# An FFT convolution kernel whose head computes the filter before it transforms the first pixels

## The chip, the core and the metric

The kernel runs on one core of a Trainium2 chip. The core has five engines that run their own instruction streams and meet through semaphores: TensorE (PE in the profile, with its weight loads shown apart as PEld), VectorE (DVE), ScalarE (ACT), GpSimd (POOL) and SyncE (SP), which here issues the DMAs. TensorE writes only into PSUM, eight banks of 512 fp32 columns on each partition; VectorE or ScalarE has to copy every result out ("evict" it) before a bank can be used again. The metric is the device time of one execution in microseconds (us).

## What is computed

The reference is a circular 7 by 7 convolution of a 224 by 224 image with 96 input and 96 output channels, written with two-dimensional FFTs:

```python
# x: (1, 224, 224, 96) bf16, w: (7, 7, 96, 96) bf16
wp = jnp.pad(w, ((0, H - K), (0, W - K), (0, 0), (0, 0)))
Xf = rfft2(x.astype(float32), axes=(1, 2))
Wf = rfft2(wp.astype(float32), axes=(0, 1))
Yf = jnp.einsum('bhwi,hwio->bhwo', Xf, Wf)
y = irfft2(Yf, s=(H, W), axes=(1, 2)).astype(bfloat16)
```

## The kernel before

The kernel does not take a full FFT. It cuts the image rows into 8 blocks of 28 (`NJ`, `B`), takes a short real transform along the rows in each block (34 input rows with overlap, 17 frequencies `s`, a real and an imaginary plane each), convolves along the columns directly in that domain, and transforms back. The columns go in 7 tiles `t` of 32.

Four kinds of work pass through TensorE.

- *The pixel transform.* `f_jobs` and `a_bank` multiply pixels (stationary, `x0_bufs` for tile 0, `xn_bufs` later) by the transform matrix `Fm` (moving) into `xf`. For tiles 0 to 2 the work is split by frequency in three parts, `SH2 = (0, 8, 13, 17)`: 8, 5 and 4 frequencies, 32 matmuls for each part and each half `jg` of the image rows, of 64, 40 and 32 columns. `xh` is the strip of six columns left of tile 0.
- *The filter transform.* `w` lies in `wq` (`wqx`) with its 49 taps on partitions, in two copies: rows 30 to 78 (first copy, all output channels) and rows 79 to 127 (second copy, shifted by 48 output channels, with the other half of the output channels in it). A matmul with `wq` as stationary operand, read with a stride of 96 elements, and a small matrix `Em` as the moving one gives the filter at some frequencies for one output channel. The first group of frequencies uses the first copy alone (`wide_jobs`, line 396: rows 0 to 78, one output channel per matmul); the others use both copies (`prep_jobs`, line 414: one matmul gives two output channels). `PGRP` lists the groups. Results go to `WF`. Of a frequency's three filter planes two are computed and the third is their difference, a VectorE instruction (`diff`, line 389).
- *The convolution.* `b_round` (line 555) handles one frequency of one tile: 33 matmuls of 96 columns (22 at the two real frequencies), with planes of `xf` and of `J` (sums and differences of `xf`, made on VectorE by `jit`, line 525) as stationary and `WF` as moving operands. Its results pass ScalarE (`tt_`), VectorE (`u`, `v`) and GpSimd (`yf`) and go to DRAM.
- *The inverse transform* (`c_jobs`), which starts much later.

The order of every engine's instructions is the order in which the Python emits them (`_Ordered`, line 91). The program has a head (lines 202 to 384 and 758 to 778) and then rounds `r`. In round `r`, tile 0 handles frequency `r` and, from round 4 on, tile 1 frequency `r - 4`. Each `b_round` has two places where other work is slipped in (`mid` and `end`), and the slots are numbered `k`: tile 0 alone has slots `2r` and `2r + 1`. `add(a, b, jobs)` spreads a list of jobs evenly over the slots from `a` to `b` (`pace`, line 785). `evac` (line 132) gives each eviction to VectorE or ScalarE by adding up estimated costs.

The head before, in order. SP issues (lines 202 to 211): tile 0's first pixel half, the first filter copy (row 49 apart, in `load_last`, the other 48 rows in one DMA), the two strips, tile 0's second half, tile 1's pixels, and last the second filter copy in four DMAs of 49 rows each. A DMA waits until the eighth before it has landed. TensorE runs 14 matmuls on zeros, transforms tile 0's first half for all 17 frequencies (96 matmuls), then runs 24 blocks of the wide filter work, each of four matmuls into one bank, 128 columns per matmul of which 110 are used (`NB0 = 4`, `NW0 = 11`), with one matmul on zeros after every fourth block (`FEV`); after block 14 (`WMID`) it puts the strips and the first part of the second half in between. Part two and three of the second half go into slots 1 to 6. VectorE and GpSimd meanwhile build `Fm`, `Em` and, on GpSimd alone, the inverse matrix `G` (`build_g`, line 339), which ScalarE and GpSimd finish at the end of the head (`g_fin`, line 777).

Of the kernel before, what the change touches and what calls it, by code (L numbers as in the profile page):

```python
# [9 lines left out]
F32 = mybir.dt.float32  # L10
# [3 lines left out]
KT = 7  # L14
# [14 lines left out]
NB0 = 4  # L29
# [4 lines left out]
PGRP = ((0, 5), (5, 8), (8, 11), (11, 14), (14, 17))  # L34
# [8 lines left out]
CQ = {2: (11, 0), 3: (11, 3), 4: (8, 7), 5: (4, 11), 6: (0, 11)}  # L43
SH2 = (0, 8, 13, 17)
# [3 lines left out]
FILL = 3  # L48
FEV = 4
WMID = 14  # L50
JIT0 = 20
W1 = 30
ZA = 1000
ZB = 3600
# [3 lines left out]
S5 = ((0, 1), (2, 3, 4), (5, 6, 11), (7, 8, 12), (9, 10, 13))  # L58
NW0 = 11


def slot(s, part):
    return S5[s][part] if s < len(S5) else 2 + 3 * (s - 1) + part


@with_exitstack
def kernel(
# [17 lines left out]
    assert K1 + PW == EP and len(S5) == PGRP[0][1]  # L85
# [26 lines left out]
    ps0_cm = tc.tile_pool(name="ps0", bufs=8, space=bass.MemoryType.PSUM)  # L112
    pools = {"psb": ps0_cm.__enter__()}
# [55 lines left out]
    Em = wqx[0:EP, WE:WE + 2 * NSLOT * NTAP].rearrange("p (h a t) -> p h a t", h=2, a=NSLOT)  # L169
# [31 lines left out]

    load_x(0, 0)
    load_last(K1 - 1, 0)
    load_w(W1, 0, PW - 1, 0)
    for jg in range(2):
        load_rows(xh_bufs[jg], jg, W - PAD, PAD)
    load_x(0, 1)
    for jg in range(2):
        load_x(1, jg)
    for i in range(4):  # L210
        load_w(K1, 0, PW, 1, i * WC // 4, (i + 1) * WC // 4)
# [5 lines left out]
    def warm(n):  # L217
        pwu = bank()
        for _ in range(n):
            TE.matmul(pwu[:].rearrange("p (a b) -> p a b", a=4), lhsT=wu[:, 0:128], rhs=wur, start=True, stop=True)  # L220
    warm(7)
    warm(7)

# [14 lines left out]
    pi_t = ftile([128, 1])  # L238
    VE.memset(pi_t[:], math.pi)
    dmy = ftile([128, 1])  # L240
    SE.activation(out=dmy[:], in_=pi_t[:], func=ACTF.Sin, bias=0.0, scale=0.0)
# [5 lines left out]
    zero_a(EP, WE // 2 + NSLOT * NTAP, 64 * C)  # L247
    zero_a(W1, 0, ZA)

# [17 lines left out]
    VE.scalar_tensor_tensor(out=tap[:], in0=ha[:], scalar=-float(PW), in1=pw_i[:], op0=ALU.mult, op1=ALU.add)  # L267
    floor_div(VE, thp[:], tap[:], KT)
# [9 lines left out]
    SE.activation(out=qq[:], in_=qq[:], func=ACTF.Sin, bias=pi_t[:], scale=-2.0 * math.pi / Q)  # L278
    zero_a(W1, ZA, ZB)

    GE.memset(mf[:], 1.0)
    GE.affine_select(out=mf[:], in_=mf[:], pattern=[[-B, JG], [0, NS * 2]], compare_op=ALU.is_ge, fill=0.0, base=-1, channel_multiplier=1)
    GE.affine_select(out=mf[:], in_=mf[:], pattern=[[B, JG], [0, NS * 2]], compare_op=ALU.is_ge, fill=0.0, base=LC, channel_multiplier=-1)
    GE.memset(mf[:, :, 2 * NS - 2:], 0.0)
# [7 lines left out]
    iota(twc[:], [[1, KT]])  # L292
    twp = ftile([EP, 1]); mk = ftile([EP, NTAP]); mk2 = ftile([EP, 2, NTAP])
    th7 = ftile([EP, 1])
    GE.tensor_single_scalar(out=th7[:], in_=thp[:], scalar=-float(KT), op=ALU.mult)
    GE.tensor_tensor(out=twp[:], in0=th7[:], in1=tap[:], op=ALU.add)
    GE.tensor_scalar(out=mk[:, 0:KT], in0=twc[:], scalar1=twp[:, 0:1], scalar2=None, op0=ALU.is_equal)
    GE.tensor_tensor(out=mk[:, KT:NTAP], in0=mk[:, 0:6:2], in1=mk[:, 1:6:2], op=ALU.add)
    VE.scalar_tensor_tensor(out=hm[:, 0:1], in0=hb[:], scalar=-2.0, in1=ha[:], op0=ALU.mult, op1=ALU.add)
    VE.scalar_tensor_tensor(out=hm[:, 1:2], in0=pw_i[:], scalar=float(PW), in1=hm[:, 0:1], op0=ALU.is_ge, op1=ALU.subtract)  # L300
    for h in range(2):
        GE.tensor_scalar(out=mk2[:, h], in0=mk[:], scalar1=hm[:, h:h + 1], scalar2=None, op0=ALU.mult)
# [4 lines left out]

# [9 lines left out]
    for r, k in ((0, KT - 1), (1, 0)):  # L317
        VE.tensor_single_scalar(out=pv[:, NS - 2, r:r + 1], in_=thp[:], scalar=float(k), op=ALU.is_equal)
# [441 lines left out]
    for p in range(3):  # L760
        for f in fj[p][0]:
            f()
# [211 lines left out]
```

## Time and profile before

| what | value |
|---|---|
| median of 3 runs (lowest, highest) | 267.96 us (267.83, 268.06) |
| the profiled execution's own time | 267.92 us |
| its span, first to last instruction | 266.1 us |
| PE busy | 254.9 us (96%), 5128 matmuls |
| DVE busy | 216.2 us (81%) |
| ACT busy | 197.3 us (74%) |
| POOL busy | 98.3 us (37%) |
| DMA | 46.78 MB, mean 176 GB/s |

Times in the views are us from the start of the span, and durations of single instructions are given in ns. A row such as `pb<-WF,J 96*128 96x96` is a matmul that writes the PSUM tile `pb` from the moving operand `WF` (96 partitions by 96 columns) and the stationary operand `J` (96 by 128). `x14` is a number of instructions, and a bracket at the end of a row says how long the engine sat idle before it and what released it. The views name all lines L101, since one helper records every instruction, so rows are told apart by their tiles.

### The profile page before, as it was taken

How to read it: one execution, taken by the hardware profiler on the slowest of the kernel's cores; microseconds unless marked ns; L12 is line 12 of the kernel's file. 1: busy time of each engine (PE TensorE's matmuls, PEld its weight loads, DVE VectorE, ACT ScalarE, POOL GpSimd, SP SyncE). 2: the span in 40 equal slices, each digit the busy share in tenths (PEclk: the TensorE clock that was granted, in tenths of full speed). 3: DMA queues.
4: the chain of work that ended last, by engine and by line, in shares of the span. 5: the costliest groups of instructions: out<-in, count | busy, mean ns of one | idle time of the engine just before them, and what ended most of it. 6: DMA issues, size and time to landing. Idle time of an engine off the chain costs nothing. (4 is left out here: it accounts for less than half of the span.)

```text
span 266.1 us, 12141 instructions
## 1 busy us (share of the span) xinstructions
PE 254.9 (96%) x5128; PEld 235.7 (89%) x5128; DVE 216.2 (81%) x465; ACT 197.3 (74%) x485; POOL 98.3 (37%) x152
## 2 busy tenths in 40 slices
PE   8997999999999999999999999999999999999992
PEld 3887999999998999999999998989999889879871
DVE  7997799889899688778887888777889889878623
ACT  8797977597964577988988789886987854178123
POOL 7781333455557344322223322233123332422100
PEclk9999999999999999999999999999999999999999
DMA  8973103711111697898876587979678533887855
GB/s 200 244 203 110 48 2 93 221 47 47 47 51 47 198 261 159 248 275 231 273 199 192 142 247 218 234 219 345 214 147 235 184 118 136 200 239 185 260 126 188
DMA packets 46786, 46.78 MB, mean 176 GB/s; under 512 B 35272, under 2 KB 38004, under 8 KB 46684
## 3 DMA queue, kind: packets, MB, share of 16 engines
q1 hardware_dynamic: 44444, 43.95, 58.8%
q10 hardware_dynamic: 2288, 2.06, 2.4%
q8 instruction: 40, 0.66, 1.1%
q14 instruction: 14, 0.11, 0.1%
HBM read 24.66 MB, written 21.33 MB: 173 GB/s over the span
## 5 line engine op out<-in xcount | busy, mean ns | idle before, releaser
L101 PE MATMUL pb<-WF,J 96*128 96x96 bf16 x2821 | 162.9, 206 | 1.7 <-DVE J L101 1.3
L101 PEld LDWEIGHTS <-J 96*128 96x128 bf16 x2821 | 138.0, 98 | 12.3 <-issue 3.5
L101 POOL TENSOR_TENSOR yf<-v,u 128x384 bf16<-128x384 f32 x79 | 81.4, 1040 | 145.3 <-issue 84.5
L101 ACT CAST xf<-pb 96x408 bf16<-96x408 f32 (+3 forms) x145 | 67.3, 487 | 6.1 <-PE pb L101 2.3
L101 PE MATMUL pb<-WF,xf 96*128 96x96 bf16 x952 | 60.0, 206 | 0.9 <-ACT WF L101 0.9
L101 DVE TENSOR_TENSOR J<-xf 96x1824 bf16<-96x1824 bf16 (+1 forms) x84 | 56.9, 716 | 0.0
L101 PEld LDWEIGHTS <-xf 96*128 96x128 bf16 x952 | 47.2, 98 | 1.4 <-issue 1.2
L101 PE MATMUL pb<-Fm,xn 118*128 118x136 bf16 (+3 forms) x640 | 45.5, 199 | 0.2 <-DVE u L101 0.2
L101 PE MATMUL pb<-tt,Gm 102*84 102x384 bf16 (+1 forms) x132 | 32.9, 326 | 0.6 <-ACT J L101 0.3
L101 ACT CAST WF<-pb 96x480 bf16<-96x480 f32 (+1 forms) x58 | 28.6, 560 | 3.1 <-PE pb L101 3.1
L101 PEld LDWEIGHTS <-xn 118*128 118x128 bf16 x640 | 30.3, 97 | 0.3 <-issue 0.3
L101 ACT CAST J<-pb 84x384 bf16<-84x384 f32 (+1 forms) x65 | 28.1, 492 | 2.6 <-PE pb L101 2.6
L101 ACT CAST yo<-pb 84x384 bf16<-84x384 f32 (+1 forms) x63 | 27.1, 488 | 2.3 <-POOL yf L101 1.3
L101 DVE TENSOR_TENSOR J<-J 96x912 bf16<-96x912 bf16 (+2 forms) x42 | 24.2, 576 | 0.0
L101 PE MATMUL pb<-wq 128*128 128x120 bf16 (+1 forms) x288 | 21.8, 226 | 1.6 <-DMA wq<-in_w_dram 1.6
L101 PEld LDWEIGHTS <-wq 128*128 128x128 bf16 (+1 forms) x288 | 19.9, 148 | 2.5 <-issue 1.2
L101 DVE TENSOR_TENSOR yf<-v,u 128x384 bf16<-128x384 f32 x26 | 15.1, 581 | 0.9
L101 PE MATMUL pb<-wu 128*112 128x384 bf16 (+1 forms) x59 | 14.7, 396 | 1.1 <-DVE ct L101 1.1
L101 PEld LDWEIGHTS <-wu 128*112 128x112 bf16 (+1 forms) x59 | 7.4, 128 | 5.8 <-issue 3.5
L101 PEld LDWEIGHTS <-Gm 102*84 102x84 bf16 (+1 forms) x132 | 11.1, 117 | 1.0 <-issue 0.4
L101 ACT COPY xf<-xf 96x816 bf16<-96x816 bf16 (+3 forms) x20 | 11.1, 616 | 0.0
L101 ACT CAST tt<-pb 112x384 bf16<-112x384 f32 x8 | 3.6, 479 | 8.7 <-PE pb L101 8.6
(387 smaller groups left out, 239.9 us busy)
## 6 DMA issues: line engine op xcount, KB each, us to landing
scr<-yf SPq DMA_DIRECT2D x30, 288.0 KB
xn<-in_x_dram SPq DMA_DIRECT2D x12, 672.0 KB
tt<-scr SPq DMA_DIRECT2D x24, 336.0 KB
out_dram<-yo SPq DMA_DIRECT2D x12, 252.0 KB
out_dram<-J SPq DMA_DIRECT2D x12, 252.0 KB
tt<-scr SPq DMA_DIRECT2D x6, 288.0 KB
WF<-in_x_dram SPq DMA_DIRECT2D x2, 672.0 KB
out_dram<-tt SPq DMA_DIRECT2D x8, 168.0 KB
```

The source lines that it names most:

```text
L101: r = fn(*a, **k)
```

## The change

The head is put in another order, and with it go other sizes.

- SP issues the first filter copy first, in three DMAs of a third of the columns each with row 49's two small DMAs between them (`load_copy`), then tile 0's first half, the strips, tile 0's second half, then the second filter copy in the same five pieces, and tile 1's pixels last.
- The wide filter group has four frequencies (`NW0 = 8` planes, 80 columns) in place of five. It is made in 8 blocks of 12 matmuls, each into a PSUM tile of two banks that one instruction evicts. The other groups are 4 to 6, 7 to 9, 10 to 12 and 13 to 16; the last has four frequencies, 160 columns per matmul and 16 blocks of three matmuls.
- `HEAD` gives the order: four wide blocks, the first pixel half, a block, a strip, a block, a strip, two blocks, the second pixel half. Only six frequencies of both halves are transformed there (`SH0`; 64 matmuls of 48 columns), evicted from two-bank tiles; the seven and the four others go to slots 0 to 3 and 8 to 11 for both halves. The head has 16 matmuls on zeros at its start and one before each block but the first.
- `Em` becomes `Em0` and `Em2`, both inside the tail of `wq`. `Em0`, `Em2` and then `Fm` are made in that order, GpSimd makes the tap masks `mk2` earlier, and the zeros of rows 0 to 29 of `wq` are written by ScalarE in halves of the output channels.
- The scratch of `build_g` lies in `J_bufs[2]`, and `g_fin` moves to round 3.
- The first `J` subtraction is cut in two (`cuts`), the `diff` of frequency 1 is an instruction in place of columns of the wide matmuls, and the slots of tile 1's first transform and of the filter groups move.

```diff
-NB0 = 4
+NB0 = 12
...
-PGRP = ((0, 5), (5, 8), (8, 11), (11, 14), (14, 17))
+PGRP = ((0, 4), (4, 7), (7, 10), (10, 13), (13, 17))
...
+SH0 = (0, 6, 13, 17)
 SH2 = (0, 8, 13, 17)
...
-FILL = 3
-FEV = 4
-WMID = 14
-JIT0 = 20
+HEAD = ("w", "w", "w", "w", "x0", "w", "h0", "w", "h1", "w", "w", "x1")
 W1 = 30
-ZA = 1000
-ZB = 3600
+ZC = 48
...
-S5 = ((0, 1), (2, 3, 4), (5, 6, 11), (7, 8, 12), (9, 10, 13))
-NW0 = 11
+S4 = ((0, 1), (2, 3, 8), (4, 5, 9), (6, 7, 10))
+NW0 = 8
...
+    psh_cm = tc.tile_pool(name="psh", bufs=4, space=bass.MemoryType.PSUM)
+    pools = {"ps": psh_cm.__enter__()}
...
 
+    def load_copy(p, h):
+        n = (C * C, WC)[h]
+        for i in range(3):
+            load_w(p, 0, PW - 1, h, i * n // 3, (i + 1) * n // 3)
+            if i == 1:
+                load_last(p + PW - 1, h)
+
+    load_copy(W1, 0)
     load_x(0, 0)
-    load_last(K1 - 1, 0)
-    load_w(W1, 0, PW - 1, 0)
     for jg in range(2):
         load_rows(xh_bufs[jg], jg, W - PAD, PAD)
     load_x(0, 1)
+    load_copy(K1, 1)
     for jg in range(2):
         load_x(1, jg)
-    for i in range(4):
-        load_w(K1, 0, PW, 1, i * WC // 4, (i + 1) * WC // 4)
...
         for _ in range(n):
-            TE.matmul(pwu[:].rearrange("p (a b) -> p a b", a=4), lhsT=wu[:, 0:128], rhs=wur, start=True, stop=True)
-    warm(7)
-    warm(7)
+            TE.matmul(pw[:, 0].rearrange("p (a b) -> p a b", a=4), lhsT=wu[:, 0:128], rhs=wur, start=True, stop=True)
+    warm(8)
+    warm(8)
...
+
+    def zero_h(h, c0, c1):
+        zv = wz[0:W1, 0:WE // 2].rearrange("p (i o) -> p i o", o=C2)[:, c0:c1, h * C2 // 2:(h + 1) * C2 // 2]
+        return SE.copy(out=zv, in_=zf[0:W1, 0:1].unsqueeze(2).to_broadcast([W1, c1 - c0, C2 // 2]))
+    zero_a(EP, WE // 2, 64 * C)
+    zero_h(0, 0, ZC)
...
-
+    SE.activation(out=qq[:], in_=qq[:], func=ACTF.Sin, bias=pi_t, scale=-2.0 * math.pi / Q)
+    zero_h(0, ZC, C)
+    late_zero = zero_h(1, 0, C)
...
+    iota(twc[:], [[1, KT]])
     GE.memset(mf[:], 1.0)
     GE.affine_select(out=mf[:], in_=mf[:], pattern=[[-B, JG], [0, NS * 2]], compare_op=ALU.is_ge, fill=0.0, base=-1, channel_multiplier=1)
     GE.affine_select(out=mf[:], in_=mf[:], pattern=[[B, JG], [0, NS * 2]], compare_op=ALU.is_ge, fill=0.0, base=LC, channel_multiplier=-1)
+    twp = ftile([EP, 1]); mk = ftile([EP, NTAP]); mk2 = ftile([EP, 2, NTAP])
+    th7 = ftile([EP, 1])
+    GE.tensor_single_scalar(out=th7[:], in_=thp[:], scalar=-float(KT), op=ALU.mult)
+    GE.tensor_tensor(out=twp[:], in0=th7[:], in1=tap[:], op=ALU.add)
+    GE.tensor_scalar(out=mk[:, 0:KT], in0=twc[:], scalar1=twp[:, 0:1], scalar2=None, op0=ALU.is_equal)
+    GE.tensor_tensor(out=mk[:, KT:NTAP], in0=mk[:, 0:6:2], in1=mk[:, 1:6:2], op=ALU.add)
+    for h in range(2):
+        GE.tensor_scalar(out=mk2[:, h], in0=mk[:], scalar1=hm[:, h:h + 1], scalar2=None, op0=ALU.mult)
...
+        VE.tensor_single_scalar(out=pv[:, NS - 2, r:r + 1], in_=thp[:], scalar=float(k), op=ALU.is_equal)
+    late = [late_zero]
+    for h in range(2):
+        late.append(VE.tensor_tensor(out=Em2[:, h].rearrange("p s (r t) -> p s r t", t=NTAP),
+                                     in0=pw3[:, N4:, 0:2].unsqueeze(3).to_broadcast([EP, NS - N4, 2, NTAP]),
+                                     in1=mk2[:, h].unsqueeze(1).unsqueeze(1).to_broadcast([EP, NS - N4, 2, NTAP]), op=ALU.mult))
     VE.tensor_tensor(out=Fm.rearrange("p r s j -> p j s r"), in0=qq[0:R, 0:JG],
                      in1=mf.rearrange("p j (s r) -> p j s r", r=2), op=ALU.mult)
...
+        at = [8]
+
+        def gtile(shape):
+            n = math.prod(shape[1:])
+            v = J2f[0:shape[0], at[0]:at[0] + n]
+            at[0] += n
+            assert at[0] <= JN // 2
+            return v.rearrange("p (j m) -> p j m", j=nj) if len(shape) > 2 else v
...
     def wide_jobs():
         ncol = NW0 * NTAP
-        wcol = 512 // NB0
-        assert ncol <= wcol and C % NB0 == 0
...
             def f():
-                pw = bank()
-                pv_ = pw[:].rearrange("p (k q) -> p k q", q=wcol)
-                ev = Em[0:K1, 0].rearrange("p a t -> p (a t)")[:, 0:wcol]
-                o0 = ob * NB0
+                pw = psum_tile()
+                ev = Em0[0:K1]
+                if ob:
+                    warm(1, pw)
                 for k in range(NB0):
-                    TE.matmul(pv_[:, k], lhsT=wqx[0:K1, o0 + k:o0 + k + 127 * C + 1:C], rhs=ev, start=True, stop=True)
-                wv = WF[0:C, 0:NW0].rearrange("i a t o -> i (a t) o")
-                apart(("W", 0), ob, evac(wv[..., o0:o0 + NB0], pv_[0:C, :, 0:ncol].rearrange("i k q -> i q k"), NB0 * ncol))
+                    o = ob * NB0 + k
+                    m = TE.matmul(pw[:, k // nk, k % nk * ncol:(k % nk + 1) * ncol], lhsT=wqx[0:K1, o:o + 127 * C + 1:C],
+                                  rhs=ev, start=True, stop=True)
+                    if (ob + 1) * NB0 <= C2:
+                        for z in late:
+                            tc.declare_no_dep(m.ins, z.ins, reason="other output channels")
+                wv = WF[0:C, 0:NW0].rearrange("i a t o -> i (a t) o")[..., ob * NB0:(ob + 1) * NB0]
+                apart(("W", 0), ob, evac(wv.rearrange("i q (b k) -> i q b k", b=2),
+                      pw[0:C, :, 0:nk * ncol].rearrange("i b (k q) -> i q b k", q=ncol), NB0 * ncol))
             return f
         return [mk_(ob) for ob in range(C // NB0)]
...
+    def head_x(jg):
+        s1 = SH0[1]
+        fv = Fm[:, :, 0:s1].rearrange("p r s j -> p r (s j)")
+        n = 2 * s1 * JG
+        for ph in range(2):
+            pa = psum_tile()
+            for k in range(TW):
+                i = 2 * k + ph
+                TE.matmul(pa[:, k // 8, k % 8 * 64:k % 8 * 64 + n], lhsT=xbuf(0, jg)[:, i * C:i * C + 128], rhs=fv, start=True, stop=True)
+            xo = xf0[0:C, ph, :, 0:s1, HALO:HALO + TW, jg * JG:(jg + 1) * JG]
+            pi = pa[0:C].rearrange("c b (w q) -> c (b w) q", q=64)[:, :, 0:n].rearrange("c w (r s j) -> c r s w j", r=2, s=s1)
+            apart(("A", 0), (0, jg, ph, 0), evac(xo, pi, TW * n))
+
+    def head_h(jg):
+        pa = psum_tile()
+        for ph in range(2):
+            a_mm(pa[:, ph], xh_bufs[jg], ph, HALO)
+        a_put(0, xf0, pa, slice(0, 2), HALO, jg, 0)
...
-        assert NB * ncol <= 512 and C2 % hb == 0
+        nb = C // (NB if 2 * ncol * (NB // 2) <= 512 else 6)
+        hb = C2 // nb
...
-        return [mk_(ob) for ob in range(nb)] + [diff(s) for s in range(s0, s1) if s not in REAL]
+        return [mk_(ob) for ob in range(nb)] + [diff(s) for s in range(s0, s1) if s not in REAL and gi > 1]
...
     def f_jobs(t, part):
-        s0, s1 = SH2[part], SH2[part + 1]
+        s0, s1 = (SH2 if t else SH0)[part:part + 2]
...
+        cuts = ((0, 1), (1, n)) if t == g == 0 else ((0, n),)
         return [
-            sub(Jb[:, 0:4, 0:n].rearrange("c (k r) s q -> c k r s q", r=2), dpl,
-                x0.unsqueeze(1).to_broadcast([C, 2, 2, n, PP]), ALU.subtract, 4 * PP * n),
+            sub(Jb[:, 0:4, a:b].rearrange("c (k r) s q -> c k r s q", r=2), dpl[:, :, :, a:b],
+                x0[:, :, a:b].unsqueeze(1).to_broadcast([C, 2, 2, b - a, PP]), ALU.subtract, 4 * PP * (b - a)) for a, b in cuts] + [
...
     xf0 = new_xf(0)
-    fj = [f_jobs(0, p) for p in range(3)]
-    for p in range(3):
-        for f in fj[p][0]:
-            f()
-    warm(FILL)
-    for i, f in enumerate(wide_jobs()):
-        if i == WMID:
-            for jg in range(2):
-                for g in a_bank(0, xf0, xh_bufs[jg], 0, 3, jg, 0):
-                    g()
-            for g in fj[0][1]:
-                g()
-        f()
-        if i == JIT0:
-            for g in jit(0, 0):
-                g()
-        if i % FEV == FEV - 1:
-            warm(1)
-    g_fin()
+    fj = [None] + [f_jobs(0, p) for p in (1, 2)]
+    load["a"] += 300
+    wj = wide_jobs()
+    for h in HEAD:
+        if h == "w":
+            wj.pop(0)()
+        else:
+            (head_x if h[0] == "x" else head_h)(int(h[1]))
+    assert not wj
+    for g in jit(0, 0):
+        g()
+    psh_cm.__exit__(None, None, None)
+    ps0_cm = tc.tile_pool(name="ps0", bufs=8, space=bass.MemoryType.PSUM)
+    pools["psb"] = ps0_cm.__enter__()
...
     for gi in range(1, len(PGRP)):
-        add(4 if gi == 1 else 2 * PGRP[gi - 1][0], 2 * PGRP[gi - 1][1] - 1, prep_jobs(gi))
+        add(3 if gi == 1 else 2 * PGRP[gi - 1][0], 2 * PGRP[gi - 1][1] - 1, prep_jobs(gi))
...
         if r == 0:
-            for i in range(2, PGRP[0][1]):
-                add(2 * i - 4, 2 * i - 3, [diff(i)])
-            add(1, 4, fj[1][1])
-            add(3, 7, fj[2][1])
+            for i in range(1, PGRP[0][1]):
+                add(max(2 * i - 3, 0), 2 * i - 1, [diff(i)])
+            for i in range(*PGRP[1]):
+                add(2 * i - 2, 2 * i, [diff(i)])
+            add(0, 4, fj[1][0] + fj[1][1])
+            add(8, 12, fj[2][0] + fj[2][1])
+        if r == 2:
+            new_xf(1, SH2[0], SH2[1])
         for p in range(3):
-            if r == (1, 3, 5)[p]:
-                new_xf(1, SH2[p], SH2[p + 1])
+            if r == (1, 3, 6)[p]:
+                if p:
+                    new_xf(1, SH2[p], SH2[p + 1])
+                else:
+                    xf_tiles[1] = xf_bufs[1]
                 fj = f_jobs(1, p)
                 if p == 2:
                     for jg in range(2):
                         fj[jg][-1] = then_load(fj[jg][-1], 2, jg)
-                add(2 * r + 1, 2 * r + (5, 5, 4)[p], fj[0] + fj[1])
+                add((4, 7, 12)[p], (7, 11, 15)[p], fj[0] + fj[1])
...
+        if r == 3:
+            g_fin()
```

## The prediction

> **What bounds the kernel now.** I read first the page's busy shares in 40 slices, which say where an engine is full; one slice is 6.65 us.
>
> ```profile
> PE   8997999999999999999999999999999999999992
> DVE  7997799889899688778887888777889889878623
> ACT  8797977597964577988988789886987854178123
> PEclk9999999999999999999999999999999999999999
> ```
>
> TensorE is full at full granted clock everywhere but at the end and in the first 30 us. Time can be won only where PE waits or does work nobody needs; work moved from the head into the rounds is paid for in full. Next, TensorE's instructions in order of time, from the head:
>
> ```profile
> 1.05 5.58 PE L101 MATMUL pb<-wu 128*128 128x512 bf16 x14 [1.05 <-DVE ct L101]
> 6.47 2.69 PE L101 MATMUL pb<-Fm,WF 118*128 118x64 bf16 x96
> 9.01 0.81 PE L101 MATMUL pb<-wu 128*128 128x512 bf16 x3
> 10.28 1.18 PE L101 MATMUL pb<-wq 79*128 79x128 bf16 x16 [0.47 <-DMA wq<-in_w_dram]
> ...
> 18.98 0.38 PE L101 MATMUL pb<-wu 128*128 128x512 bf16 x1
> 20.26 0.50 PE L101 MATMUL pb<-WF,xf 96*128 96x96 bf16 x8 [0.90 <-ACT WF L101]
> ...
> 26.35 0.92 PE L101 MATMUL pb<-wq 128*128 128x120 bf16 x12 [1.11 <-DMA wq<-in_w_dram]
> 27.10 0.63 PE L101 MATMUL pb<-Fm,xn 118*128 118x64 bf16 x16
> ```
>
> The first convolution starts at 20.26, after waiting 0.90 us for the last eviction of wide filter work; at 26.35 PE has waited 1.11 us for the second filter copy. Starts divided by counts give the prices (the durations overlap). Third, stretches by engine:
>
> ```profile
> core 0: us, PE busy (x) PEld busy (x) DVE busy (x) ACT busy (x) POOL busy (x), PEclk, DMA share, GB/s
> 8.00:17.00 9.00, 8.53 (x166) 7.64 (x163) 8.78 (x17) 7.09 (x16) 7.14 (x29) 1.00 0.98 249
> 17.00:25.00 8.00, 7.10 (x170) 6.73 (x169) 6.16 (x13) 7.01 (x19) 3.33 (x7) 1.00 0.43 144
> 26.30:33.50 7.20, 7.15 (x174) 7.18 (x175) 5.38 (x11) 6.40 (x15) 2.35 (x2) 1.00 0.12 44
> ```
>
> From 17 to 25 us, when the second copy moves, the DMA engines are only 43% busy, against 98% before it. In the early rounds (last row) PE is full although ACT is 89% busy.
>
> **A, first convolution earlier: -2.3 us.** The 14 matmuls on zeros end at 6.47; the last run at 0.22 us each, so 16 end at 6.9. By then the weights are there: the first pixel DMA (0.69 MB) had landed at 5.72, when the DMA that had to wait for it issued; 0.9 MB now starts at the same time, in five issues of about 0.6 us, and 0.95 MB had moved by 5 us at the rates shown for single microseconds (55, 178, 356, 356 GB/s). Zeros: ScalarE's 1036 columns took 1.04 us; the new order needs about 2690 before the sine and 1150 after it, ending near 6.5. `Em0` follows the sine by some 0.9 us of small VectorE instructions (0.15 to 0.25 each), near 6.2.
>
> From 6.9, PE alone counts. A wide matmul cost 62.5 ns at 128 columns (16 in 0.99 us) and the same at 120 (12 in 0.75); contiguous pixels of 136 columns cost 60, of 64 columns 28.8, of 40 columns 25.6. As two widths cost the same, I charge the strided weight load and keep 62.5 at 80 columns. So: 96 x 62.5 ns = 6.0; seven matmuls on zeros at 0.22 = 1.5; 64 transforms of 48 columns at 26.7 ns (between the 40 and 64 rows) = 1.7; 12 strip matmuls at 60 ns = 0.7. Sum 9.9, end at 16.8. Evictions: ScalarE took 529 ns for 440 elements and 607 for 512, so 1.09 us for 960 and 0.89 for 768; VectorE 610 and 678, so 1.10 and 0.92. No two-bank eviction is in the trace; by one fixed part per bank it would cost 0.05 to 0.2 more, off the path but for the last. Eight wide, four pixel and two strip evictions make some 7 us on each of two engines, beside 9.9 us of PE. The last wide block ends at 15.9, its eviction at 17.0, and that of the second half behind it at 17.9: first convolution at 17.95. The second half lands by 14 (3.5 MB had moved by 15.5, and it is in the first 2.7).
>
> **B, second copy: -1.1 us.** It now goes ahead of tile 1's pixels in 48 rows, as the first copy did, and is 3.5 MB deep in the queue: by 16 to 17 us. Its first use comes at 22. The 1.11 us goes. Tile 1's pixels land by about 21 if the 249 GB/s hold, and are needed at 24.4. Should the 43% not be the 49 rows' doing, they come at 26.3 as now: 1.9 us late.
>
> **C, transforms moved: +1.8 us.** In the rounds, tile 0 had 64 matmuls at 25.6 ns (1.6 us); now 64 of 56 columns at 27.7 and 64 of 32 at 25.6 (3.4 us).
>
> **D, +0.4 us.** The last filter group's 48 matmuls have 160 columns: 70 ns by the slope from 64 to 136, against 62.5.
>
> **E, evictions in rounds 0 to 3: 0 to +1.9, I take +0.4.** From 17.95 PE has 12.2 us of work to the end of round 3, with 30 evictions (8 of tile 0's second part, 12 filter, 10 of tile 1). Low end: from 26.35 to 33.54 PE ran unbroken through 21 such evictions, 2.9 per us against 2.5 wanted. High end: VectorE also has `J` three times, five `diff` (646 ns each), `u` and `v`, about 10.6 of the 12.2 us, and ScalarE 3.0 us of its own (halo copies, `tt_`, the moved sine of 0.38). That leaves room for 22 evictions; five can wait in banks, three cost 0.27 each (0.8), and the `u` of round 2 stands behind seven evictions and two halo copies on ScalarE, `J`'s third instruction behind four evictions on VectorE, and PE's third filter part behind that: another 1.1. The nearest row is the before's own rounds with the same mix, so I stay near the low end.
>
> Nothing is charged for `g_fin` (POOL's 0.78 us in its idle time, needed at round 3's `J`), the cut `J` instruction (VectorE is otherwise waiting for PE), or `diff` of frequency 1 apart from E; without that cover each is 0.4 to 0.8.
>
> Sum: -2.3 - 1.1 + 1.8 + 0.4 + 0.4 = -0.8. Span 266.1 - 0.8 = 265.3, plus the 1.8 that lies outside the span in the profiled execution (267.92): 267.1. That execution is 0.04 below the median, which changes nothing.
>
> **Rivals.**
>
> *Columns set the price of a wide matmul.* For it: pixels go by their columns from 64 on. Against it: 120 and 128 cost the same. Then 80 columns cost 36 ns (28.8 plus 16 columns at 0.434), the blocks 2.5 us less. The second half's arrival near 14, its 0.9 us and its eviction then set the first convolution at about 15.9: 265.1.
> [...]
>
> *What the head gains the rounds give back.* E at 1.2 to 1.7: 267.9 to 268.4, no change. For it: ACT is 89% busy in the nearest window without the added evictions.
>
> *The evicting engines become the bound (slower).* Place: rounds 2 and 3, where 12 evictions fall in 4.3 us. ScalarE's queue is in order, so `tt_` waits behind evictions, `u` behind `tt_`, and the banks behind both. It decides once E passes 1.8, where the other terms' 1.2 and the 0.54 us that a measurement can tell (0.2%) are used up. E of 1.9 to 2.6 gives 268.6 to 269.3. Against it: the window at 26.3.
>
> *Transfers set the pace.* The first copy lands at 8.5, not 6.5, or pixels at 26.3. Each costs 1.6 to 1.9: 268.7 to 269.0. Against it: 356 GB/s at 3 to 5 us.
> [...]
>
> **How the numbers follow.** Forecast 0.44 (its own range 266.5 to 267.6), columns 0.13, given back 0.18, evictions 0.14, transfers 0.11. 0.2% is 0.54 us: under 267.4 lie the columns and 0.38 of the forecast, 0.51; within, the rest of the forecast and the give-back, 0.24; above, 0.25. The range from 265.1 to 268.8 leaves out the ends of the two slower rivals and part of the columns, under 0.2.
>
> **What would show it.** A: first `WF,xf` matmul at 17.5 to 18.4, 96 `wq` matmuls of 80 columns in 6.0 us. B: no PE wait for `wq` after 20 us. C: the `Fm,WF` rows. E: PE idle released by ACT or DVE between 18 and 33 us, 0.1 to 0.8 in total. I am wrong if the first `wq` matmul starts after 7.5, if its spacing is near 36 ns, or if that idle passes 1.8.

## The result, and the profile after

The changed kernel takes 277.56 us (median of 6 executions, 276.24 to 278.48) against 267.89 us (267.04 to 269.02) for the kernel before beside it: a ratio of 1.0354 [1.0327, 1.0381], 9.7 us slower. The forecast was 267.1 us. The profiled execution took 276.24 us with a span of 274.5 us, 8.4 us longer than the span before. It is the fastest of the six and lost the least clock (a mean granted clock of 0.994, the others 0.978 to 0.988), so what the profile shows below is 8.4 of the 9.7 us.

The busy shares in 40 slices, of the changed kernel (one slice is now 6.86 us):

```profile
PE   8979899998769999999999999999999999999993
...
ACT  8768887779943567898997979888897864268113
...
PEclk9999999999997999999999999999999999999999
```

Slices 10 to 13 (62 to 89 us) are new: PE falls to 8 and 7 tenths while ScalarE is full, then to 6 when ScalarE is down to 4, and in the thirteenth slice the granted clock falls. The head is not where the time went. TensorE's instructions in order of time, of the changed kernel (start, duration, engine, operation, tiles, count, and in brackets the idle time before and what ended it):

```profile
6.88 0.88 PE L98 MATMUL ps<-wq 79*128 79x80 bf16 x12 [0.27 <-DVE wq L98]
7.58 0.39 PE L98 MATMUL ps<-wu 128*128 128x512 bf16 x1
...
17.82 0.50 PE L98 MATMUL pb<-WF,xf 96*128 96x96 bf16 x8 [1.31 <-DVE xf L98]
...
24.67 0.84 PE L98 MATMUL pb<-wq 128*128 128x120 bf16 x10 [0.39 <-issue]
...
80.84 0.34 PE L98 MATMUL pb<-WF,J 96*128 96x96 bf16 x4 [1.71 <-DVE J L98]
...
82.45 1.30 PE L98 MATMUL pb<-WF,J 96*128 96x96 bf16 x25 [0.93 <-DVE J L98]
```

The first convolution starts at 17.82 (20.26 before), the 1.11 us wait for the second filter copy is gone, and the large waits are those for `J` near 81 us. The stretches by engine, of the changed kernel and then of the kernel before:

```profile
core 0: us, PE busy (x) PEld busy (x) DVE busy (x) ACT busy (x) POOL busy (x), PEclk, DMA share, GB/s
18.00:22.00 4.00, 3.61 (x103) 3.49 (x100) 3.87 (x8) 2.94 (x8) 1.80 (x3) 1.00 1.01 242
60.00:70.00 10.00, 8.29 (x163) 7.73 (x160) 7.05 (x14) 9.07 (x15) 4.35 (x4) 1.00 0.08 31
70.00:80.00 10.00, 8.09 (x174) 7.51 (x170) 6.73 (x13) 8.42 (x14) 2.33 (x2) 1.00 0.09 33
82.00:84.00 2.00, 1.55 (x31) 1.55 (x32) 1.60 (x5) 0.98 (x3) 2.00 (x2) 0.87 0.00 0
84.00:86.00 2.00, 2.00 (x37) 2.00 (x36) 1.55 (x4) 0.96 (x3) 0.90 (x2) 0.50 0.38 147
86.00:88.00 2.00, 2.00 (x44) 2.00 (x42) 0.78 (x2) 0.38 (x2) 1.40 (x4) 0.77 0.00 0
```

```profile
60.00:70.00 10.00, 10.00 (x237) 10.00 (x233) 9.13 (x19) 8.09 (x19) 5.93 (x6) 1.00 0.09 33
70.00:80.00 10.00, 10.00 (x246) 10.00 (x245) 8.56 (x18) 7.42 (x19) 4.91 (x5) 1.00 0.17 63
```

From 60 to 100 us TensorE idles 5.76 us (40 less 34.24 busy), before 0.44 (40 less 39.56). From 82 to 88 the clock costs 0.26 + 1.0 + 0.46 = 1.7 us. Together that is 7.0 of the 8.4 us; the other 1.4 are not broken down here. What happens there is the last filter group, frequencies 13 to 16. ScalarE in order of time, and VectorE beside it, both of the changed kernel:

```profile
61.26 0.42 ACT L98 ACTIVATE tt__1796<-pb 128x288 f32<-128x288 f32 x1 [0.93 <-PE pb L98]
61.57 3.49 ACT L98 CAST WF<-pb 96x480 bf16<-96x480 f32 x4
64.83 0.65 ACT L98 CAST xf<-pb 96x512 bf16<-96x512 f32 x1
65.36 0.43 ACT L98 ACTIVATE tt__1869<-pb 128x288 f32<-128x288 f32 x1
```

```profile
70.02 0.36 DVE L98 SCALAR_TENSOR_TENSOR u<-pb,tt__1943 128x192 f32<-128x192 f32 x1 [1.79 <-ACT tt__1943 L98]
...
74.03 0.36 DVE L98 SCALAR_TENSOR_TENSOR u<-pb,tt__2017 128x192 f32<-128x192 f32 x1 [2.66 <-ACT tt__2017 L98]
```

Four filter evictions of 0.9 us stand on ScalarE between one `tt_` and the next, so `tt_` comes late, `u` waits for it up to 2.66 us, and the banks, `v` and `J` follow. In the kernel before, three evictions of 1.46 us together stand between two `tt_`, and the longest such wait of `u` in its last filter group (65 to 75 us) is 0.62 us:

```profile
70.26 0.36 DVE L101 SCALAR_TENSOR_TENSOR u<-pb,tt__2110 128x192 f32<-128x192 f32 x1 [0.62 <-ACT tt__2110 L101]
```

The groups by form between 58 and 92 us give the price, in the kernel before and in the changed one:

```profile
L101 ACT CAST WF<-pb 96x480 bf16<-96x480 f32 x17 | 8.3, 565 | 0.0
```

```profile
L98 ACT CAST WF<-pb 96x480 bf16<-96x480 f32 x15 | 13.2, 1062 | 0.0
...
L98 DVE CAST WF<-pb 96x480 bf16<-96x480 f32 x1 | 0.9, 917 | 0.0
```

The same engine copies the same 96 by 480 elements of the same types in 1062 ns in place of 565. Neighbouring copies overlap in these records (15 of 1062 ns in 13.2 us busy), so a copy's share of ScalarE's time is the busy time divided by the count: 0.88 us (13.2 / 15) in place of 0.49 (8.3 / 17). What differs is not in the row: `hb` is 3 in the last group, so three neighbouring output channels are written together, then a jump; it was 4.

### The profile page after: what moved, and what is told of

It reads as the page before. It is cut to its first block, busy times and chain, and to the rows that moved or that the text cites. A ratio compares the mean times of both kernels' runs of the same rounds, so it can differ in the third digit from the quotient of the medians.

```text
span 274.5 us, 12123 instructions
## 1 busy us (share of the span) xinstructions
PE 258.0 (94%) x5128; PEld 238.0 (87%) x5128; DVE 214.8 (78%) x459; ACT 202.3 (74%) x474; POOL 98.2 (36%) x152
## 5 line engine op out<-in xcount | busy, mean ns | idle before, releaser
L98 ACT CAST xf<-pb 96x408 bf16<-96x408 f32 (+4 forms) x137 | 64.4, 489 | 5.6 <-PE pb L98 1.9
L98 PE MATMUL pb<-WF,xf 96*128 96x96 bf16 x952 | 60.8, 207 | 1.9 <-DVE xf L98 1.3
L98 DVE TENSOR_TENSOR J<-xf 96x456 bf16<-96x456 bf16 (+3 forms) x85 | 55.6, 694 | 0.1
L98 ACT CAST WF<-pb 96x480 bf16<-96x480 f32 x46 | 28.6, 725 | 0.5 <-PE pb L98 0.5
L98 PEld LDWEIGHTS <-wq 128*128 128x128 bf16 (+1 forms) x288 | 20.6, 151 | 3.4 <-issue 2.1
L98 PE MATMUL pb<-wq 128*128 128x120 bf16 (+1 forms) x192 | 16.0, 227 | 1.6 <-ACT WF L98 1.0
L98 DVE TENSOR_TENSOR WF<-WF 96x960 bf16<-96x960 bf16 x15 | 10.2, 714 | 0.1
```

Source lines behind the costliest of these rows:

```text
L98: r = fn(*a, **k)
```

## The experiments

**The price of an eviction by itself.** A kernel of copies alone, from one PSUM bank to tiles with written runs of 2 to 6 bf16, six copies each on ScalarE and on VectorE.

```python
dst = d[0:C, :, :, o:o + k]        # k neighbours, then a jump
src = pb[0:C, 0:q * h * k].rearrange("i (k h q) -> i q h k", h=h, q=q)
```

> This kernel computes none of the reference: it copies x to the output and repeats evictions from PSUM, fp32 to bf16, six times on ScalarE and six on VectorE for each shape, with different numbers of neighbouring bf16 elements in the destination (runs of 2, 3, 4, 5, 6; run3odd starts at an odd element; run3short has fewer elements; run3flat and run4flat read PSUM in order). Theory 'run of three': 480 elements in runs of 3 take 0.85 us or more on ScalarE and 0.9 on VectorE, against 0.57 and 0.65 in runs of 4, and the flat reads show the same, so that the destination decides. Rival 'load': runs of 3 and 4 differ by under 5%, and the long evictions in the changed kernel come from what runs beside them.

Groups by form in this kernel (`flat` reads PSUM in order, `odd` starts at the fourth element, `short` has 360 elements; the digit of a plain `run` is not shown, so the fence leaves its 480-element groups out, and they are told apart by their place in time):

```profile
L42 ACT CAST run3odd<-pb 96x480 bf16<-96x480 f32 x6 | 5.5, 912 | 5.9 <-DVE run L44 5.7
L51 ACT CAST run3flat<-pb 96x480 bf16<-96x480 f32 x6 | 5.5, 911 | 4.3 <-DVE run L44 4.2
L53 DVE CAST run3flat<-pb 96x480 bf16<-96x480 f32 x6 | 5.5, 911 | 5.9 <-ACT run3flat L51 5.7
...
L42 ACT CAST run3short<-pb 96x360 bf16<-96x360 f32 x6 | 4.3, 722 | 5.9 <-DVE run3odd L44 5.7
L53 DVE CAST run4flat<-pb 96x480 bf16<-96x480 f32 x6 | 3.9, 653 | 3.7 <-ACT run4flat L51 3.6
L42 ACT CAST run<-pb 96x320 bf16<-96x320 f32 x6 | 3.3, 555 | 4.7 <-DVE run3short L44 4.6
L51 ACT CAST run4flat<-pb 96x480 bf16<-96x480 f32 x6 | 3.3, 555 | 5.9 <-DVE run3flat L53 5.7
```

Runs of three cost 912 ns against 555 for runs of four or six on ScalarE, and 911 against 653 on VectorE. Where the run starts and in which order PSUM is read changes nothing. Runs of two are dear too (320 elements, 555 ns), five lie in between (636 on ScalarE). Why three costs so much was not found.

**Runs of three in the kernel before.** The kernel before with the last group alone in 16 blocks of three.

```diff
-        nb = C // NB
-        hb = NB // 2
+        nb = C // (6 if gi == 4 else NB)
+        hb = C2 // nb
```

> The kernel before, with one part alone: its last filter group (frequencies 14 to 16) in 16 blocks of three matmuls in place of 12 of four, so that each eviction writes 360 elements in runs of three. Theory 'run of three': the 16 evictions take 0.7 us or more each, ScalarE carries 4 to 6 us more between 65 and 90 us, and the time rises by 2 to 7 us. Rival 'load': the evictions take 0.46 us and the time stays within 0.6 us.

It takes 271.36 us, a ratio of 1.0111 [1.0035, 1.0187]. The 16 evictions, of only 360 elements, take 832 ns on ScalarE, and TensorE is busy 8.64 of the 10 us from 70 to 80 (10.00 before). Three per block is enough to lose 3 us without any other part of the change.

**Two per block in the changed kernel.**

```diff
-        nb = C // (NB if 2 * ncol * (NB // 2) <= 512 else 6)
+        nb = C // (NB if 2 * ncol * (NB // 2) <= 512 else 4)
```

> The changed kernel, with its last filter group in 24 blocks of two matmuls, so that each eviction writes 320 elements in runs of two. Theory 'run of three': the 24 evictions take about 0.43 us each, 10.3 us in place of some 16, and the time falls to 269 to 273 us. Rival 'load' (too many evictions in too few slots on ScalarE): 24 are more than 16, the time stays at 277 or rises.

273.95 us, a ratio of 1.0187 [1.0103, 1.027]. There are 24 evictions of 320 elements at 627 ns on ScalarE: shorter ones, but runs of two. By busy time one costs 0.46 us (21 in 9.6 us), near the 0.43 expected. About 3.6 us come back and the rest stays: the time is just above the 269 to 273 expected.

**Six per block.** The last group cut in two of two frequencies: the same 16 evictions of 480 elements, in runs of six.

```diff
-PGRP = ((0, 4), (4, 7), (7, 10), (10, 13), (13, 17))
+PGRP = ((0, 4), (4, 7), (7, 10), (10, 13), (13, 15), (15, 17))
...
-        nb = C // (NB if 2 * ncol * (NB // 2) <= 512 else 6)
+        nb = C // (NB if ns == 3 else 12)
```

> The changed kernel with its last filter group cut into two of two frequencies each (13, 14 and 15, 16), in the same slots: 16 evictions of 480 elements as before, but six matmuls of 80 columns in each, so that six neighbouring channels are written together in place of three. TensorE has 48 matmuls more: 96 at 57 ns in place of 48 at 70, +2.1 us. If the length of the written run is what makes these evictions slow: each takes 555 to 600 ns on ScalarE in place of about 1000, and the kernel takes 269.5 to 271.0 us (268.2 of the version with five frequencies first, plus 2.1, plus up to 0.7 of waits). If it is their number, their size or their place in rounds 10 to 13: 277 to 280 us, the changed kernel's time plus up to the 2.1.

```profile
L98 ACT CAST WF<-pb 96x480 bf16<-96x480 f32 x15 | 7.5, 576 | 0.0
```

576 ns, as expected, and 273.95 us (ratio 1.025 [1.0215, 1.0284]): 3.6 us less than the changed kernel although TensorE has 48 matmuls (about 2.1 us) more. But not the 269.5 to 271.0 expected: two waits for `J` (0.63 and 0.93 us, from 78.5 us on) and the clock's fall (0.83 on average from 80 to 90 us) remained. So the length of the run sets the price of these evictions, but it is not all of the loss.

**The slow evictions shared between two engines.** The changed kernel with the last group's evictions dealt in turn.

```diff
+                if gi == 4:
+                    load["va"[ob % 2]] += 800
+                    apart(("W", gi), ob, (VE.tensor_copy, SE.copy)[ob % 2](out=wo, in_=pi))
```

> The changed kernel with the last filter group's 16 evictions dealt in turn to VectorE and ScalarE, in place of 15 on ScalarE. If they hurt through ScalarE's queue alone (tt_ waits behind them): ScalarE is relieved of about 7 us in rounds 10 to 13, and the time is 269 to 273 us. If a slow eviction costs the same wherever it runs (VectorE took 911 ns for it too, and has J, u and v to do): 275 us or more.

275.74 us, a ratio of 1.031 [1.0277, 1.0342]. ScalarE falls to 7.43 and 5.92 busy of 10 in the two stretches from 60 to 80 us, and VectorE goes to 10.00 in both. So the loss does not come from ScalarE's queue alone: dealt evenly, the evictions fill VectorE, which has `J`, `u` and `v` to do as well, while ScalarE has 6.65 of the 20 us to spare. An uneven split was not tried.

**The crowd ahead of `J`.** In the changed kernel three subtractions (`diff` of frequencies 13, 14, 15, 1.86 us) stand on VectorE right ahead of the `J` that TensorE waits for at 80.84. Here two of them come in rounds 13 and 14.

```diff
-... if s not in REAL and gi > 1]
+... if s not in REAL and gi > 1 and s < 14]
...
+    add(26, 27, [diff(14)])
+    add(28, 29, [diff(15)])
```

> The changed kernel with the third filter planes of frequencies 14 and 15 (two VectorE subtractions of 0.62 us each) made in rounds 13 and 14, when they are first needed, in place of all three at the end of round 12, right ahead of the J of tile 1's next frequencies. If those subtractions are what makes J late and the granted clock fall: PE's two waits for J near 81 us (1.71 and 0.93 us) shrink by about 1.2, the clock stays at 1.0 from 82 to 88 us (2.2 us), and the time is 273.5 to 275.0 us. If J is late because of the evictions alone, or the clock falls anyway: 276.5 to 278 us.

276.16 us, a ratio of 1.0302 [1.0235, 1.037]. The first wait for `J` shrinks from 1.71 to 0.57 us, as expected; the second stays at 0.93, and the clock falls all the same (0.84, 0.50, 0.80 from 82 to 88 us). The time lies between the two ranges expected. It is 1.4 us under the changed kernel's, but the two intervals overlap, so with the slow evictions still there this repair alone is not clear of noise.

**Both repairs, and the wait in the head filled.** Six per block and the two late subtractions (first run), and the same with five matmuls on zeros at the end of the head (second run).

```diff
     assert not wj
+    warm(5)
```

> Both repairs: the last filter group cut in two with runs of six channels, and the two late subtractions in rounds 13 and 14. If slow evictions and the crowd ahead of J are all of the loss: 270.3 to 271.6 us, which is the five-frequency version's 268.2 plus 2.1 for the 48 matmuls more, plus up to 1.3 of waits, at a granted clock of 1.0 from 78 to 88 us. If something else of the four-frequency layout costs: 273 us or more.

> Both repairs of the last filter group, and five matmuls on zeros at the end of the head, where TensorE waited 1.31 us. If the spread of the repaired version (272.3 at a mean clock of 0.997 to 274.3 at 0.984) is the granted clock's fall after that wait: all executions are at 0.994 or more, and the median is 271.0 to 272.5 us. If not: 273 us or more, with some executions at 0.985.

With both repairs no wait of TensorE between 60 and 86 us is over 0.3 us in the trace and the clock stays at 1.00 from 70 to 90, as expected. The time is 273.13 us all the same (ratio 1.0201 [1.0141, 1.0261]), above the 270.3 to 271.6 expected: now the clock fell in the head. With the wait filled the time is 271.88 us (1.0161 [1.0115, 1.0207]) and the mean clock of every execution 0.996 or more, where two of four had 0.984 and 0.985. That is four executions of each, so it speaks for the wait at the end of the head as what sets off the fall, and does not prove it. The 271.88 us are still 1.6 above the 270.3 that the five-frequency version (next) and the 48 matmuls give together; 0.6 of it is a longer stop near 25 us (1.07 against 0.46 us, see below), and the rest is open. The stretches of the changed kernel with late subtractions show it right behind that wait (1.31 us before 17.91):

```profile
18.00:20.00 2.00, 2.00 (x41) 2.00 (x41) 2.00 (x5) 1.18 (x3) 1.27 (x3) 0.63 0.98 237
20.00:22.00 2.00, 2.00 (x36) 2.00 (x34) 1.60 (x3) 0.96 (x2) 0.00 (x0) 0.52 1.07 243
```

The clock costs 0.74 + 0.96 = 1.7 us here. In the profile of the changed kernel (first row of its stretches above) the same wait left the clock at 1.00: the same idle time costs nothing in one execution and 1.7 us in another.

The traces' own record of the clock says more. In the 15 traces of the convolution, up to the kernel's last microseconds, the clock is at half rate for 3.41 us or for twice that, and each fall comes a whole number of 3.41 us after the clock's first rise, which lies 4.0 to 6.8 us behind the start of the span. In the changed kernel the rise is at 4.99 us and the fall 78.51 us later, 23 times 3.41; the falls of the last microseconds, 259.41 us after the rise in the kernel before and 269.65 in the changed one, are 76 and 79 times. The stretch before the changed kernel's one fall, and the fall:

```profile
80.09:83.50 3.41, 1.73 (x37) 1.59 (x38) 3.03 (x7) 0.49 (x2) 2.58 (x3) 1.00 0.00 0
83.50:86.91 3.41, 3.41 (x57) 3.41 (x54) 2.29 (x6) 1.53 (x5) 2.08 (x4) 0.50 0.22 87
```

So, as far as these traces show it, a fall goes with the idle time within one such stretch, all its waits added up, and where the stretch begins differs from trace to trace (the rise at 5.93 us in the kernel before, at 4.99 in the changed one). Before the ten falls TensorE was busy for 36 to 71% of the stretch (51% here). Every stretch at full clock that was under 60% busy was followed by a fall, none over 71% was, and between the two both happened: in five kernels the stretch that holds the whole wait of 1.31 us was 62% busy, and in one of them, that with the late subtractions, a fall followed.

**The grouping as a whole.** The changed kernel with five frequencies in the first group and three in each later one, so that all later evictions have runs of four: 12 wide blocks of eight matmuls, 100 columns each.

```diff
-NB0 = 12
+NB0 = 8
...
-PGRP = ((0, 4), (4, 7), (7, 10), (10, 13), (13, 17))
+PGRP = ((0, 5), (5, 8), (8, 11), (11, 14), (14, 17))
...
-NW0 = 8
+NW0 = 10
```

> The changed kernel with the first filter group back at five frequencies (ten planes, 100 columns, 12 blocks of eight matmuls with two-bank evictions of 800 elements; the other groups of three frequencies with runs of four, as before the change); the order of the head, the loads and the slots of the transforms stay as changed. Theory 'run of three': the loss between 60 and 87 us goes, and the time is 266.3 to 268. Rival 'moved transforms': the loss stays, 275 or more.

268.17 us, a ratio of 0.9994 [0.9964, 1.0024]. The grouping, with its group of four at the end, is the whole loss, and all the rest of the change is worth nothing that can be told.

**The second filter copy alone.** The kernel before with one part of the change.

```diff
+    for i in range(3):
+        load_w(K1, 0, PW - 1, 1, i * WC // 3, (i + 1) * WC // 3)
+        if i == 1:
+            load_last(K1 + PW - 1, 1)
     for jg in range(2):
         load_x(1, jg)
-    for i in range(4):
-        load_w(K1, 0, PW, 1, i * WC // 4, (i + 1) * WC // 4)
```

> The kernel before with one part of the change: the second filter copy goes ahead of tile 1's pixels, in three DMAs of 48 rows with row 49 apart, in place of four of 49 rows behind them. If the prediction's step B holds: PE's wait of 1.11 us for the second copy goes, no wait for tile 1's pixels takes its place, and the time is 266.6 to 267.2 us. If the wait is hidden or turns into one for pixels or for an evicting engine: 267.7 to 268.5 us.

It is slower, outside both expectations: 270.67 us, 1.0088 [1.0055, 1.0121]. The wait for `wq` is gone; a longer one stands earlier, with no cause that the profile names, and the clock falls behind it. TensorE in order of time, and the stretches:

```profile
23.09 0.41 PE L101 MATMUL pb<-Fm,WF 118*128 118x40 bf16 x10
25.39 0.53 PE L101 MATMUL pb<-Fm,WF 118*128 118x32 bf16 x14 [1.89 <-issue]
```

```profile
24.00:26.00 2.00, 0.61 (x19) 0.61 (x19) 2.00 (x4) 0.04 (x1) 0.00 (x0) 0.74 0.13 41
26.00:28.00 2.00, 2.00 (x33) 2.00 (x31) 0.09 (x1) 1.51 (x3) 0.99 (x1) 0.50 0.03 8
28.00:30.00 2.00, 2.00 (x29) 2.00 (x28) 0.82 (x2) 1.45 (x4) 0.00 (x0) 0.50 0.00 0
30.00:32.00 2.00, 2.00 (x30) 2.00 (x28) 1.24 (x4) 1.12 (x3) 0.00 (x0) 0.55 0.00 0
```

The stop falls inside a block, two matmuls into it, where there is nothing to wait for. The clock costs 0.52 + 1.0 + 1.0 + 0.9 = 3.4 us. Two of its seven executions kept a mean clock of 1.0 and took 268.4 and 268.7 us: that is the price of a stop of 1.89 us for a wait of 1.11. The others lost more to the clock.

**What the stop is.** The same stop, 0.39 us, is in the changed kernel (the row at 24.67). Four runs with five frequencies first ask what it is: the second pixel half and `J` ahead of the last two wide blocks; the same without the 11 matmuls on zeros between the blocks; the same with the second copy in three DMAs of 49 rows; and without the 11, but with four such matmuls at the end of the head. The first line of the diff is in all four, the second in the second and fourth, the third in the third and the last in the fourth.

```diff
-HEAD = ("w",) * 6 + ("x0", "w", "w", "h0", "w", "h1", "w", "w", "w", "x1")
+HEAD = ("w",) * 6 + ("x0", "w", "w", "h0", "w", "h1", "w", "x1", "j", "w", "w")
...
-                if ob:
-                    warm(1, pw)
...
-    load_copy(K1, 1)
+    for i in range(3):
+        load_w(K1, 0, PW, 1, i * WC // 3, (i + 1) * WC // 3)
...
     assert not wj
+    warm(4)
```

> The version with five frequencies in the first filter group, with the second pixel half transformed ahead of the last two wide blocks, and J's first instructions on VectorE between them. If VectorE's work at the start of round 0 is what gives the head's gain back: 267.0 to 267.9 us. If the rounds' evictions as a whole give it back: 268.2 us within 0.3.

> The five-frequency version with the second pixel half ahead of the last two blocks, without the 11 matmuls on zeros between the wide blocks (22 instructions of TensorE fewer ahead of everything that follows). If the stop near 25 us is TensorE's code arriving late: it falls at the same instruction number, 694 to 698, which is now inside tile 1's first pixel transform and no longer in the filter block, and it ends 2.6 to 2.9 us after a 16 KB packet of the instruction queue has started; the head's gain of up to 2.4 us goes into it and the time is 267.0 to 268.0 us. If it is a wait for data of the filter block: it stays in front of the second matmul of that block, and the time is the same as with the fillers.

> The same five-frequency version (with its fillers), with the second filter copy in three DMAs of 49 rows in place of 48 rows and row 49 apart, still ahead of tile 1's pixels. If full DMA engines hold TensorE's code back: with part of the engines free the 16 KB packet starts by 21.5 us (20.4 in the kernel before, 22.6 with 48 rows), the stop of 1.34 us shrinks to under 0.5, and the time is 266.5 to 267.4 us, unless the pixels, now behind a slower copy, make TensorE wait instead (up to 268.5). If the DMA engines' load has nothing to do with it: the stop stays at 1.0 us or more.

> The five-frequency version without fillers between the wide blocks, with four matmuls on zeros at the end of the head instead, where TensorE waited 1.18 us for the last eviction (four take 0.88 us). If that wait is what made the granted clock fall there (0.62 from 17 to 21 us): the clock stays at 1.00, the mean clock is 0.995 or more in nearly all executions, and the median is 266.2 to 267.0 us, like the one execution without fillers that had a clock of 1.0 (266.27). TensorE then reaches instruction 694 before its code is there: a stop that ends at about 25 us, now after the first one to three matmuls of tile 1's pixel transform. If the clock falls for another reason, the median stays at 267.6 to 268.3 us, with executions between 266 and 270. If the stop is a wait for the filter block's data, it lies in front of that block's second matmul as before.

The first takes 267.83 us (0.9993 [0.9975, 1.001]), with a stop of 1.34 us in place of 0.46: whatever the head gains, the stop takes, for it ends at 25.2 in both. The second, 268.01 us (1.0017 [0.9985, 1.005]), did not answer, because the clock fell to 0.62 behind a wait in the head and TensorE came to the place late, without a stop. The third has no stop, but waits for tile 1's pixels instead (0.48 and 0.41 us): 268.67 us, 1.0039 [1.0005, 1.0073]. It came to the place only at about 25.0 us (23.9 in the first), so it does not test the stop. The fourth moved the stop as expected, but at 268.43 us (1.0003 [0.9972, 1.0033]) it missed the 266.2 to 267.0 expected. It and the repaired kernel with its filled wait, in order of time, one after the other:

```profile
22.57 0.64 PE L98 MATMUL pb<-wq 128*128 128x120 bf16 x8
25.35 1.46 PE L98 MATMUL pb<-Fm,xn 118*128 118x64 bf16 x24 [2.15 <-DVE WF L98]
```

```profile
23.67 0.29 PE L98 MATMUL pb<-WF,J 96*128 96x96 bf16 x3
25.03 0.33 PE L98 MATMUL pb<-WF,J 96*128 96x96 bf16 x4 [1.07 <-issue]
```

Counted in TensorE's own program, the stop comes after instruction 692 to 696 in each: after 692 with five frequencies (both orders of the head, the fourth run too) and in the repaired kernel, 694 in the changed one, 696 with the copy alone. The work standing there is a filter block, tile 0's transform, tile 1's transform or a convolution. (The 2.15 us are put down to VectorE's `WF`, the last semaphore that this matmul waits for; the place and the end are those of the others.) What the kernels share is a queue of instructions. The DMA queues on the changed kernel's page (packets, MB, share of the engines):

```profile
q8 instruction: 40, 0.66, 1.0%
```

The packets have 16 KB each and come in step with TensorE: from the start of the second to that of the last it starts 9,542 of its 10,256 matmuls and weight loads, 251 to a packet on average, from 146 to 388 (253 in the kernel before). That they hold TensorE's instructions is read from this and from the times that follow. The packet that matters, the second, starts at 20.5 us in the kernel before, at 21.95 in the changed one, and at 22.4 to 22.8 where the stop is 0.46 us or longer. Nine kernels have the stop (also the changed one with runs of two, with shared evictions and with runs of six, after instruction 694: 0.72, 0.54 and 0.19 us), and in each of them TensorE goes on 2.5 to 2.8 us after the packet's start. In the kernel before it would have gone on between 23.0 and 23.3, and got there only at about 23.4: no stop. With 49-row DMAs the packet starts at 20.3, as in the kernel before. So all rows fit TensorE's code arriving late behind the data. What is in the packet, which engine carries it, and when it is asked for, no trace here shows, and no run moved the packet alone.

No version beats the kernel before. The fourth run's best executions took 266.9 us, but eight of its twelve had a mean clock under 0.995, and in the profiled one it fell behind the 2.15 us stop; delaying some of the data so that the code passes was not tried.

## Why the prediction was wrong

**A, first convolution earlier: right.** 17.82 against 17.95 predicted. The wide blocks were cheaper (12 matmuls in 0.69 us, 58 ns each at 80 columns, between the 62.5 charged and the rival's 36), so TensorE was done at 16.51 and not at 16.8. The last eviction did not move with it: the sum left TensorE 1.15 us to wait there, and it waited 1.31. The two misses nearly cancel, so that 17.82 is so near is partly luck. That the wait can be followed by a fall of the clock was not in the sum.

**B, second copy: right in what goes, wrong in what covers it.** The 1.11 us went, and the rival "transfers set the pace" fell: data were in time. The step took the 43% to be the 49 rows' doing, and no run shows why rows should matter; with 48 the share was 1.01 from 18 to 22 us, and with 49 in their place TensorE waited for tile 1's pixels (0.48 and 0.41 us, third of the four runs on the stop). But by the reading above TensorE's code then came late behind the data (the second packet at 21.95 us, 20.5 before). In the changed kernel it cost 0.39 us. Alone the edit is 3 us slower, not 1.1 faster. The 43% load of the engines was read as slack to be used; by this reading part of it was what let the code through.

**C: right. E: inside its range, but three times what was taken.** Sixteen matmuls of 56 columns took 0.42 us and sixteen of 32 columns 0.41, about 26 ns each, as C charged. TensorE's idle time between 18 and 33 us that VectorE releases is 0.39 + 0.20 + 0.34 + 0.24 = 1.2 us, where E took 0.4: over the 0.8 given but under the 1.8 at which E would have failed. The window from 26.35 us on which E's low end rested holds 18 starts of evictions in the trace, not 21: 2.5 per us, just the rate wanted, so it showed less room than was read from it. The five-frequency version has A, B, C and E without D and comes to no change, where the sum of those four had -1.2: the head's gain is given back, the rival that had 0.18, though part of it goes into the stop (0.46 us there), which that rival did not name.

**D is the step that failed.** It charged the last filter group's 48 matmuls with 0.4 us for wider columns and nothing for their evictions, whose form the change also alters. Twelve blocks of four became 16 of three. ScalarE spends 13.2 us and VectorE 0.9 on them, where twelve at 0.49 us are 5.9. ScalarE has no room for that in rounds 10 to 12, and an even split fills VectorE instead. TensorE idles 5.3 us more, and behind its longest waits the clock falls for another 1.7.

**The slower rival** had the mechanism, `tt_` behind evictions, `u` behind `tt_`, the banks behind both. It was placed in rounds 2 and 3, where the number of evictions rises, and not where their price does. So its size (up to 2.6) was too small, and the range's upper end lies 8.8 us under the result.

## What to carry to other kernels

When a change alters how many results share a bank, work out the new output pattern of its evictions first: the shape in the profile does not show it, and the length of the written run can cost more than the number of elements (on ScalarE 722 ns for 360 elements in runs of three, 555 for 480 in runs of four). A wait that is taken away is worth only the time to the next thing that is late, and by the reading above TensorE's own code was one of the things that can be (a stop of 1.89 us for a wait of 1.11). Idle time of TensorE was to be counted twice in these runs when it added up to some 1.4 us within 3.41 us (each stretch at full clock under 60% busy was followed by a fall): once as it stands, and once for the 1.7 or 3.4 us that the clock cost behind it. Below that it went either way: a wait of 1.34 us had no fall behind it, one of 1.31 us had one in some executions.

## What the runs showed of the hardware

- Evictions of fp32 from PSUM to bf16 in SBUF, 480 elements on 96 partitions: 555 ns on ScalarE in runs of four or six, 636 in runs of five, 912 in runs of three; on VectorE 653 to 656 in runs of four, five and six, and 911 in runs of three. In the kernel, where neighbouring copies overlap, runs of three take 0.88 us of ScalarE's time each and runs of four 0.49.
- The granted clock fell to 0.50 behind waits of 1.89 and 2.15 us and behind 1.71 + 0.93; behind a wait of 1.31 us it fell in some executions and not in others. All ten falls came at a whole number of 3.41 us after the clock's first rise, behind a stretch of 3.41 us in which TensorE was busy for 36 to 71%. Each fall cost either 1.7 us (82 to 88 us in the changed kernel, 18 to 22 with late subtractions) or 3.4 us (24 to 32 with the copy alone, 80 to 88 with shared evictions), which is half rate for 3.4 or 6.8 us.
- TensorE stopped inside a block, by the reading above for its own code: 0.19 to 2.15 us in nine kernels, each time after instruction 692 to 696 and 2.5 to 2.8 us after a packet of the instruction queue started (in the changed kernel after 694, 0.39 us, 2.72 us after). The profile then names "issue", or the semaphore that happens to come last.
